# A conditional block for overflow jobs placed ahead of the last two scatters, and layer 1's accumulators in the branches moved to other PSUM tags

## The chip, the cores and the metric

The kernel runs on one core of a Trainium2 chip. The metric is the device time of one execution in microseconds (us), lower is better. Engines are named as in the profile: PE (TensorE; PEld is its weight load), DVE (VectorE), ACT (ScalarE), POOL (GpSimd), SP (SyncE, which only issues transfers here). A "q" behind a name (POOLq) is the engine's sequencer, which issues the instructions, waits on semaphores and takes branches.

## The reference

Retention attention (4 batches, 8 heads, 768 positions, head width 64) gives 3072 rows of 512. They go through a mixture of 8 experts in which each row takes the one expert with the highest logit:

```python
logits = x @ w_gate                       # 3072 x 8
expert_idx = np.argmax(logits, axis=1)
gate_w = softmax(logits)[row, expert_idx]
for e in range(E):                        # rows lo:hi of expert e, after sorting by expert
    h = np.maximum(x_sorted[lo:hi] @ w1[e], 0.0)    # 512 -> 1024
    y_sorted[lo:hi] = h @ w2[e]                     # 1024 -> 512
y = gate_w[:, None] * y_sorted[inv_perm]
```

## The kernel before

The first part, up to about 139 us, is attention and routing. The rows of `x` go to a scratch tensor in DRAM; the routing tables say, for each expert, which rows to gather and to which output rows its results are scattered. Nothing of that part is changed.

The second part is a loop over the eight experts (`for e in range(E)`), written in a hand-made order on all engines (`tc.manual_schedule`). Each expert has up to 512 places. Per expert:

- `tc.Switch(which, ARMS, ...)` (L742) branches on the number of rows in steps of 8. Only PE and ACT have code in its arms. An arm is one call of `job`: eight times `layer1` (PE products `hp` at L215, then a ReLU by ACT at L217 that writes `hT`), then `layer2` (PE products `ye` at L228, then ACT copies and scalings at L233, L234 and L236) for the rows beyond the first 256. A tile with 65 to 96 rows is done in two pieces, and a piece of up to 32 rows is laid over four column groups: its ACT part is then four copies (L233) and one scaling (L234).
- After the switch, `pair` (L258 and following) does the first 256 rows of the expert before (from e = 2 on; after the last switch it runs twice, for experts 6 and 7) with one level of Strassen's scheme: seven products `yp` (L266) in three PSUM accumulators `ya`, `yb`, `yc`. ACT scales some of them (`m` at L281, `o` at L290), DVE combines the rest (L272).
- POOL scatters the finished tiles to the output with indirect DMAs (`scatter`, L298) and gathers the rows of the expert after next; DVE transposes them (L206) and prepares sums and differences for the next `pair`.

PSUM has eight banks, given out by tag: `sc` (2), `lg` (1), `tr` (3), `y` (2). In `pair`, `ya` and `yb` take `sc`, and `yc` takes `tr`. In `layer1` the tag goes by the number of the block `f`:

```python
    hp_tags = [("sc", 2), ("sc", 2), ("lg", 1), ("tr", 3)]
    ...
        hp = ps(*hp_tags[f % len(hp_tags)], "hp")[:, 0:n]
```

An instruction that takes a bank waits, through a semaphore, until the last reader of that bank is done. Each engine counts its finished instructions in one semaphore. Where the reader stands in a switch, the count at which it is done differs from arm to arm, and one wait stands for all arms.

At the very end there is a block that is run only if some expert has more than 512 rows (not so with these inputs): `with tc.If(more > 0): further_jobs()` (L774), with `more` read into a register on every engine at L746. Where the block is not run, each engine still has a few instructions in its place, which bring the semaphores to the values that the block would have left: event semaphores on all engines, and on POOL an `INC_SWDGE_SEM`, which first waits until every scatter before it has landed. L797 is the end of the program: SP waits for all transfers, each engine drains, and POOL collects the others in a barrier.

Of the kernel before, what the change touches and what calls it, by code (L numbers as in the profile page):

```python
# [52 lines left out]
def kernel(  # L53
# [11 lines left out]
    nc = tc.nc  # L65
    B, H, S, D = q.shape
    N, DM = out.shape
    E = w_gate.shape[1]
# [5 lines left out]
    W = 512  # L74
    TC = W // P
    EARLY = 256
# [9 lines left out]
    def ps(tag, bufs, name):  # L86
        return psum.tile([P, 512], F32, tag=tag, name=name, bufs=bufs)
# [119 lines left out]
                    xT[ts(g, L), :, 0 : n * P].rearrange("p a (t r i) -> p r t a i", r=Q, i=L)[:, r, :, :, :],  # L207
                    xs[ts(r, L), tiles[0] : tiles[0] + n, ts(g, P)].rearrange("p t (a i) -> p t a i", i=L))

    hp_tags = [("sc", 2), ("sc", 2), ("lg", 1), ("tr", 3)]  # L210

    def layer1(n, xT, w1t, hT, f):
        hp = ps(*hp_tags[f % len(hp_tags)], "hp")[:, 0:n]
        for dt in range(DT):
            nc.tensor.matmul(hp, lhsT=w1t[:, 0, dt, ts(f, P)], rhs=xT[:, dt, 0:n], start=(dt == 0),  # L215
                             stop=(dt == DT - 1))
        nc.scalar.activation(out=hT[:, f, 0:n], in_=hp, func=AF.Relu)  # L217
# [78 lines left out]
    def scatter(o, idx, tiles):  # L296
        for t in tiles:
            done = nc.gpsimd.indirect_dma_start(  # L298
                out=out[:, :], out_offset=bass.IndirectOffsetOnAxis(ap=idx[:, t : t + 1], axis=0), in_=o[:, t, :],
                in_offset=None, bounds_check=N - 1, oob_is_err=False)  # L300

            tc.declare_no_dep(done.ins, group="scatters", reason="other rows of the output")
            tc.add_to_no_dep_group("scatters", done.ins)
# [32 lines left out]
    with ExitStack() as actx:  # L336
# [231 lines left out]
        xTa = first.tile([P, DT, EARLY], F32, tag="xTa", name="xTa")  # L568
        xT1 = first.tile([P, DT, W], F32, tag="xT1", name="xT1")
        hTa = keep.tile([P, FT, EARLY], F32, tag="hTa", name="hTa")  # L570
        oa = keep.tile([P, EARLY // P, DM], F32, tag="oa", name="oa")
        rest = iter(())
        for n in range(len(steps)):
            if n + AHEAD < len(steps):
                load(n + AHEAD)
            if n == len(steps) - 3:
                wa = weights(first, 0)
# [27 lines left out]
        for t in range(HALF):  # L605
            tr = ps("tr", 3, "tre").rearrange("p (a t) -> p a t", a=DT)
# [2 lines left out]
            nc.vector.tensor_copy(xTa[:, :, ts(t, P)], tr)  # L609
        next(rest, None)  # L610
        for f in range(FT):
            layer1(EARLY, xTa, wa[0], hTa, f)
            if f in (0, 1, 3):
                next(rest, None)
            if f == 2:
                ne = count()
        src, dst, gates = tables(inv, "", lambda rows: [gather(xs2[e], rows[:, ts(e, TC)], range(HALF, TC)) for e in range(2)])
        cols = [(src[:, ts(e, TC)], dst[:, ts(e, TC)], gates[:, ts(e, TC)]) for e in range(E)]
        arm, over = arms(ne)
# [14 lines left out]
    o2 = [keep2.tile([P, TC, DM], F32, tag=f"o{i}", name=f"o{i}") for i in range(2)]  # L634
# [23 lines left out]
        return xT  # L658

    def further_jobs():  # L660

        with tc.tile_pool(name="op", bufs=1) as op:

            def ot(shape, name, dt=F32):
                return op.tile(shape, dt, tag=name, name=name)


            jobs_i, jobs, jend, jbeg = ot([P, E], "jobs_i", I32), ot([P, E], "jobs"), ot([P, E], "jend"), ot([P, E], "jbeg")
            nc.vector.tensor_scalar(out=jobs_i, in0=ne, scalar1=float(W - 1), scalar2=float(W), op0=ALU.add, op1=ALU.max)
            nc.vector.tensor_single_scalar(jobs_i, jobs_i, W.bit_length() - 1, op=ALU.arith_shift_right)  # L670
            nc.vector.tensor_scalar(out=jobs, in0=jobs_i, scalar1=-1.0, scalar2=None, op0=ALU.add)
            ones_e = ot([P, E], "ones_e")
            nc.gpsimd.memset(ones_e, 1.0)
            nc.vector.tensor_tensor_scan(jend, ones_e, jobs, 0.0, op0=ALU.mult, op1=ALU.add)
            nc.vector.tensor_tensor(out=jbeg, in0=jend, in1=jobs, op=ALU.subtract)
            nth = ot([P, OV], "nth")
            nc.gpsimd.iota(nth, pattern=[[1, OV]], base=0, channel_multiplier=0, **exact)
            mine, whose_f, whose = ot([P, NT, E], "mine"), ot([P, OV], "whose_f"), ot([P, OV], "whose", I32)
            past = mine[:, 0:OV, :]
            nc.vector.tensor_tensor(out=past, in0=inner(nth[:, :], E), in1=middle(jend[:, :], OV), op=ALU.is_ge)  # L680
            nc.vector.tensor_reduce(whose_f, past, axis=AX.X, op=ALU.add)
            nc.vector.tensor_scalar(out=whose, in0=whose_f, scalar1=float(E - 1), scalar2=None, op0=ALU.min)


            blk, jf, big = ot([P, NT], "blk", I32), ot([P, NT], "jf"), ot([P, NT], "big")
            nc.vector.tensor_single_scalar(blk, ranks, W.bit_length() - 1, op=ALU.arith_shift_right)
            nc.vector.tensor_tensor(out=mine, in0=ohs, in1=middle(jbeg[:, :], NT), op=ALU.mult)
            nc.vector.tensor_reduce(jf, mine, axis=AX.X, op=ALU.add)
            nc.vector.tensor_tensor(out=jf, in0=jf, in1=blk, op=ALU.add)
            nc.vector.tensor_scalar(out=big, in0=blk, scalar1=1.0, scalar2=None, op0=ALU.is_ge)  # L690
            nc.vector.tensor_tensor(out=jf, in0=jf, in1=big, op=ALU.mult)
            nc.vector.tensor_scalar(out=jf, in0=jf, scalar1=-1.0, scalar2=None, op0=ALU.add)
            col, prow = ot([P, NT], "ocol", I32), ot([P, NT], "oprow", I32)
            nc.vector.tensor_single_scalar(prow, ranks, P - 1, op=ALU.bitwise_and)
            nc.vector.tensor_single_scalar(col, ranks, W - 1, op=ALU.bitwise_and)
            nc.vector.tensor_single_scalar(col, col, P.bit_length() - 1, op=ALU.arith_shift_right)
            slot, slots = ot([P, NT], "slot"), ot([P, OV * TC], "slots")
            nc.gpsimd.iota(slots, pattern=[[1, OV * TC]], base=0, channel_multiplier=0, **exact)
            nc.vector.scalar_tensor_tensor(out=slot, in0=jf, scalar=float(TC), in1=col, op0=ALU.mult, op1=ALU.add)
            at = ot([P, NT, OV * TC], "oat")  # L700
            val = ot([P, NT, 5, OV * TC], "oval", BF16)
            nc.vector.tensor_tensor(out=at, in0=middle(slots[:, :], NT), in1=inner(slot[:, :], OV * TC), op=ALU.is_equal)

            for i in range(5):
                nc.vector.tensor_tensor(out=val[:, :, i, :], in0=at, in1=inner(told[:, :, i], OV * TC), op=ALU.mult)
            here = ot([P, NT, P], "ohere", BF16)
            nc.vector.tensor_tensor(out=here, in0=middle(rrow[:, :], NT), in1=inner(prow[:, :], P), op=ALU.is_equal)
            found = ps("tr", 3, "ofound")[:, 0 : 5 * OV * TC]
            for n in range(NT):
                nc.tensor.matmul(found, lhsT=here[:, n, :], rhs=val[:, n, :, :].rearrange("p a s -> p (a s)"),  # L710
                                 start=(n == 0), stop=(n == NT - 1))
            got = ot([P, 5, OV * TC], "got")
            nc.vector.tensor_copy(got[:, :, :].rearrange("p a s -> p (a s)"), found)
            osrc, odst, ogates = tables(got, "_o")
            fetch = [nc.sync.value_load(whose[0:1, j : j + 1], min_val=0, max_val=E - 1) for j in range(OV)]
        for j, ev in enumerate(fetch):
            w1t, w2t = weights(first, ev)
            xT = mp.tile([P, DT, W], F32, tag="xTs", name="oxT")
            hT = mp.tile([P, FT, W], F32, tag="hT", name="ohT")
            gather(xs2[j % 2], osrc[:, ts(j, TC)], range(TC))  # L720
            turn(xs2[j % 2], xT, range(TC))
            for f in range(FT):
                layer1(W, xT, w1t, hT, f)
            for t in range(TC):
                layer2(W, hT, w2t, o2[j % 2], t, ogates[:, ts(j, TC)])
            scatter(o2[j % 2], odst[:, ts(j, TC)], range(TC))

    with tc.manual_schedule(engines={PE, ACT, POOL, DVE, SP}):
        for t in o2:
# [3 lines left out]
        for e in range(E):  # L733
# [8 lines left out]
            for a in tc.Switch(which, ARMS, hint=f"job{e}"):  # L742
                n = max(STEP * (LEAST + a) - (0 if e else EARLY), STEP)
                job(n, xT, w1s[e], w2s[e], hT, o2[e % 2], cols[e][2], HALF if e else 0, hint if e < 2 else lambda: None)
            if last:
                more = nc.values_load(over[0:1, 0:1], min_val=0, max_val=1)  # L746
            else:
                xT, which = xTn, nxt
            if last:
                end = halves_of_h(hT, mp.tile([P, DT, W], F32, tag="xTs", name="xTs")), end  # L750
            for d in [e - 1] * (e > 1) + [e] * last:
                pair(hTs[d], w2s[d], *(end if d == e else sums), o2[d % 2], cols[d][2],
                     lambda: None if last else hint())
                if d < e:
                    scatter(o2[e % 2], cols[e][1], range(HALF, TC))
                scatter(o2[d % 2], cols[d][1], [1, 0])
                if d + 2 < E:
                    w2s.append(weights2(homes[d % 2], d + 2))
# [10 lines left out]
            if e + 2 < E:  # L769
                xTn = rows_of(e + 2)  # L770
            if e + 2 == E:

                end = halves_of_w(w2s[E - 1], [x[:, 2 * i : 2 * i + 2, :].rearrange("p a d -> p (a d)") for x in xs2 for i in range(2)])
    with tc.If(more > 0):  # L774
        further_jobs()


# [23 lines left out]
```

## Time and profile before

| what | value |
|---|---|
| four runs | 490.22, 490.65, 491.77 and 495.67 us; median 491.21 |
| profiled execution | 490.91 us; span from first to last instruction 489.0 us |
| granted TensorE clock, mean | 0.992 |
| PE busy, whole span | 465.1 us (95%) |
| PE busy, 184 to 300 us | 116.0 of 116 us |
| PE busy, 300 to 340 us | 37.95 of 40 us |
| PE busy, 340 to 478 us | 137.18 of 138 us |
| PE busy, 478 to 489 us | 0 of 11 us |
| POOL busy, 478 to 489 us | 0.98 us |

The first row says how far runs lie apart; the second ties the trace to a time: 1.9 us lie outside the span. The rows by stage say where PE has no gap (so that only less PE work or a faster PE would help) and where it has.

### The profile page before, as it was taken

To read this page: it belongs to the slowest core of one execution; us is meant where nothing else is said; L and a number is where in the kernel's file an instruction comes from. 1 tells how busy PE (TensorE), PEld (TensorE's weight loads), DVE (VectorE), ACT (ScalarE), POOL (GpSimd) and SP (SyncE) were. 2 spreads that over 40 slices of the span, in tenths; PEclk is the share of its full clock that TensorE was granted. 3 is DMA by queue.
4 is the path that set the end of the run, shared out by engine and by line. 5 is a ranking of instruction groups with operands and counts; after the bars stand their busy time and mean duration, and the time that the engine had idled before them with its cause. 6 is when DMAs were issued, how large, how long until landed. Compare 5 with 4: busy or idle time off the path is not lost.

```text
span 489.0 us, 8236 instructions
## 1 busy us (share of the span) xinstructions
PE 465.1 (95%) x3238; PEld 320.1 (65%) x3238; DVE 260.2 (53%) x551; ACT 106.4 (22%) x218; POOL 133.8 (27%) x132
## 2 busy tenths in 40 slices
PE   7999999998989999999999999989999999999990
PEld 4778778786767565555585557658557766755880
DVE  3468776787778920765525714383481636550310
ACT  2343333332221112212211120131131121012110
POOL 2772533441303124033026012411501511100211
PEclk9999999999999999999999999999999999999996
DMA  9998999792961089343009202901910570320011
GB/s 210 217 229 204 225 236 218 171 199 70 340 195 41 25 300 364 132 135 133 3 28 353 93 26 78 380 17 39 365 56 30 168 290 21 123 95 3 26 46 46
DMA packets 93498, 72.52 MB, mean 148 GB/s; under 512 B 53466, under 2 KB 78042, under 8 KB 93408
## 3 DMA queue, kind: packets, MB, share of 16 engines
q1 hardware_dynamic: 88144, 58.74, 42.3%
q0 software_dynamic: 5120, 12.60, 7.3%
q8 instruction: 48, 0.79, 0.7%
q14 instruction: 42, 0.34, 0.2%
q10 hardware_dynamic: 144, 0.05, 0.0%
HBM read 60.88 MB, written 14.68 MB: 155 GB/s over the span
## 4 chain that ended last, share of the span: by engine, by line
PE 85%; DVE 9%; ACT 1%; issue 1%; DMA 1%; POOL 0%; SPq 0%; DVEq 0%; POOLq 0%; ACTq 0%
PE hp L215 35%; PE yp L266 17%; PE ye L228 16%; PE y L440 4%; PE sc L411 4%; DVE am L413 3%; PE tr L371 2%; PE y L435 2%; PE new L422 2%; PE warm L344 1%; DVE xg L447 1%; DMA x_d<-xg 1%; PE parts L459 1%; DVE told L522 1%; PE lgp L469 1%
## 5 line engine op out<-in xcount | busy, mean ns | idle before, releaser
L215 PE MATMUL hp<-xTs,w1t 128*128 128x392 f32 (+5 forms) x384 | 127.4, 492 | 0.0
L215 PEld LDWEIGHTS hp<-xTs,w1t 128*128 128x128 f32 x384 | 73.0, 190 | 52.5 <-issue 30.1
L206 DVE STREAM_TRANSPOSE xTs<-xs 32x512 f32<-32x512 f32 x96 | 67.5, 703 | 62.9 <-DMA xs<-x_d,src 36.3
L298 POOL DMA_INDIRECT out_dram<-o,dst x30 | 33.9, 1129 | 228.2 <-ACT o L236 135.3
L228 PE MATMUL ye<-w2t,hT 128*8 128x128 f32 (+6 forms) x496 | 66.4, 360 | 0.0
L217 ACT ACTIVATE hT<-hp 128x392 f32<-128x392 f32 (+6 forms) x64 | 29.2, 468 | 143.0 <-PE hp L215 116.5
L228 PEld LDWEIGHTS ye<-w2t,hT 128*8 128x8 f32 (+6 forms) x496 | 32.6, 123 | 31.6 <-issue 29.0
L165 POOL DMA_INDIRECT xs<-x_d,src x28 | 37.6, 1343 | 24.6 <-DVE at L188 16.4
L413 DVE TENSOR_TENSOR am<-sc,causal 128x512 f32<-128x512 f32 x48 | 30.7, 681 | 17.9 <-PE sc L411 17.9
L272 DVE SCALAR_TENSOR_TENSOR u<-yp,gate,m 128x256 f32<-128x256 f32 x14 | 6.8, 484 | 57.3 <-ACT m L281 29.7
L385 POOL TENSOR_TENSOR vs<-v,dec 128x512 f32<-128x512 f32 x23 | 24.5, 1069 | 32.1 <-PE y L440 16.2
L266 PE MATMUL yp<-ws,hs 128*128 128x256 f32 x144 | 32.1, 379 | 0.0
L440 PE MATMUL y<-am,vs 128*64 128x128 f32 x384 | 29.3, 279 | 2.6 <-DVE am L413 2.2
L382 POOL TENSOR_TENSOR qs<-q,dec 128x512 f32<-128x512 f32 x22 | 22.5, 1044 | 29.4 <-DMA q<-in_q_dram 29.4
L266 PEld LDWEIGHTS yp<-ws,hs 128*128 128x128 f32 x144 | 27.4, 190 | 3.7
L411 PE MATMUL sc<-qT,kT 64*128 64x128 f32 x384 | 27.9, 285 | 1.4 <-ACT qT L399 0.7
L266 PE MATMUL yp<-w2t,hT 128*128 128x256 f32 x112 | 26.5, 380 | 2.0 <-ACT o L234 2.0
L440 PEld LDWEIGHTS y<-am,vs 128*64 128x64 f32 x384 | 22.0, 136 | 8.2 <-DVE am L413 4.1
L411 PEld LDWEIGHTS sc<-qT,kT 64*128 64x128 f32 x384 | 23.3, 187 | 5.2 <-issue 2.7
L266 PEld LDWEIGHTS yp<-w2t,hT 128*128 128x128 f32 x112 | 21.2, 190 | 7.3 <-issue 2.4
L442 ACT COPY xTg<-y 128x512 f32<-128x512 f32 x24 | 14.1, 587 | 49.5 <-PE y L440 44.5
L215 PE MATMUL hp<-xTa,w1t 128*128 128x256 f32 (+1 forms) x128 | 22.5, 330 | 0.8 <-DVE xTa L609 0.5
(169 smaller groups left out, 525.7 us busy)
## 6 DMA issues: line engine op xcount, KB each, us to landing
w1t<-in_moe_w_dram SPq DMA_DIRECT2D x8, 2048.0 KB, 17.6
w2t<-in_moe_w_dram SPq DMA_DIRECT2D x8, 2048.0 KB
k<-in_k_dram SPq DMA_DIRECT2D x24, 256.0 KB, 5.2
q<-in_q_dram SPq DMA_DIRECT2D x12, 512.0 KB, 7.0
v<-in_v_dram SPq DMA_DIRECT2D x24, 256.0 KB, 5.7
x_d<-xg SPq DMA_DIRECT2D x24, 256.0 KB, 4.3
out_dram<-o,dst POOLq DMA_INDIRECT x30, 3.3
xs<-x_d,src POOLq DMA_INDIRECT x28, 4.7
```

The costliest lines, as they stand in the source:

```text
L165: nc.gpsimd.indirect_dma_start(out=xs[:, t, :], out_offset=None, in_=x_d[0:rows, :], in_offset=bass.IndirectOffsetOnAxis(ap=idx[:, t : t + ...
L206: nc.vector.transpose(xT[ts(g, L), :, 0 : n * P].rearrange("p a (t r i) -> p r t a i", r=Q, i=L)[:, r, :, :, :], xs[ts(r, L), tiles[0] : t ...
L215: nc.tensor.matmul(hp, lhsT=w1t[:, 0, dt, ts(f, P)], rhs=xT[:, dt, 0:n], start=(dt == 0), stop=(dt == DT - 1))
L217: nc.scalar.activation(out=hT[:, f, 0:n], in_=hp, func=AF.Relu)
L228: nc.tensor.matmul(y[j * z : j * z + m, 0:c], lhsT=hT[:, f, t * P + r0 : t * P + r0 + m], rhs=w2t[:, 0, f, ts(j, c)], start=(f == 0), stop ...
L266: nc.tensor.matmul(y, lhsT=a[:, f, :], rhs=b[:, f, :], start=start and f == 0, stop=f == FH - 1, skip_group_check=True)
L298: done = nc.gpsimd.indirect_dma_start(out=out[:, :], out_offset=bass.IndirectOffsetOnAxis(ap=idx[:, t : t + 1], axis=0), in_=o[:, t, :], i ...
L382: mul.tensor_tensor(out=qs[:, e, :, :], in0=got["q"][:, :, ts(e, D)], in1=inner(dec[:, ts(c + e, H)], D), op=ALU.mult)
L385: mul.tensor_tensor(out=vs, in0=got["v"], in1=inner(dec[:, ts(NC + c, H)], D), op=ALU.mult)
L411: nc.tensor.matmul(sc[j][:, a, :], lhsT=kT[r, a, :], rhs=qT[r, a, :], start=True, stop=True)
L413: nc.vector.tensor_tensor(out=am[j], in0=sc[j], in1=middle(causal[:, :], HP), op=ALU.mult)
L440: nc.tensor.matmul(y[ts(j, D), a, :], lhsT=vs[:, 2 * a + j, :], rhs=am[j][:, a, :], start=(c == 0), stop=True, skip_group_check=True)
```

## The change

Three edits:

1. `layer1` has an argument with its tags. Inside the branches it takes `lg`, `tr`, `tr`, `tr` in turn; the one call outside (the first 256 rows of expert 0, ahead of the loop) passes the old list.
2. `further_jobs()` and its `tc.If` stand inside the last turn of the loop, after the last `pair` and ahead of the last two scatters, with `preferred_fallthrough_block=False`, which puts the code of the case "not run" directly behind the compare and the block behind that. `further_jobs` uses the output tile `o2[E % 2]`, that is `o2[0]`, which the last two scatters (of `o2[1]`) don't read.
3. `more` is read at the end of the turn e = 6 rather than after the last switch.

```diff
-    hp_tags = [("sc", 2), ("sc", 2), ("lg", 1), ("tr", 3)]
-
-    def layer1(n, xT, w1t, hT, f):
-        hp = ps(*hp_tags[f % len(hp_tags)], "hp")[:, 0:n]
+    def layer1(n, xT, w1t, hT, f, tags=(("lg", 1), ("tr", 3), ("tr", 3), ("tr", 3))):
+        hp = ps(*tags[f % len(tags)], "hp")[:, 0:n]
...
-            layer1(EARLY, xTa, wa[0], hTa, f)
+            layer1(EARLY, xTa, wa[0], hTa, f, (("sc", 2), ("sc", 2), ("lg", 1), ("tr", 3)))
...
-                layer2(W, hT, w2t, o2[j % 2], t, ogates[:, ts(j, TC)])
-            scatter(o2[j % 2], odst[:, ts(j, TC)], range(TC))
+                layer2(W, hT, w2t, o2[E % 2], t, ogates[:, ts(j, TC)])
+            scatter(o2[E % 2], odst[:, ts(j, TC)], range(TC))
...
-            if last:
-                more = nc.values_load(over[0:1, 0:1], min_val=0, max_val=1)
-            else:
+            if not last:
                 xT, which = xTn, nxt
...
                 if d < e:
                     scatter(o2[e % 2], cols[e][1], range(HALF, TC))
+                if d == e:
+                    with tc.If(more > 0, preferred_fallthrough_block=False):
+                        further_jobs()
                 scatter(o2[d % 2], cols[d][1], [1, 0])
...
             if e + 2 == E:
+                more = nc.values_load(over[0:1, 0:1], min_val=0, max_val=1)
...
-    with tc.If(more > 0):
-        further_jobs()
```

## Prediction

> **What bounds the kernel now.** First the busy time by stage (columns: us, then busy time and count of PE, PEld, DVE, ACT, POOL, then clock, DMA share, GB/s):
>
> ```profile
> 300.00:340.00 40.00, 37.95 (x223) 27.69 (x222) 21.23 (x30) 8.22 (x19) 11.04 (x9) 1.00 0.41 146
> 340.00:478.00 138.00, 137.18 (x595) 91.08 (x593) 61.32 (x85) 22.81 (x49) 28.31 (x23) 1.00 0.31 112
> 478.00:489.00 11.00, 0.00 (x0) 0.00 (x0) 0.00 (x0) 0.00 (x0) 0.98 (x1) 0.62 0.11 41
> ```
>
> In the loop over the experts PE is the bound: it has no gap from 340 us to its end at 477.2, at a granted clock of 1.00. An edit that takes no PE work away can gain in two places only: the 2.05 us that PE misses between 300 and 340 us, and the 11 us after PE's end, in which one 0.98 us instruction is all that any engine computes.
>
> The timeline shows the first place (start, length, engine, line, operation, count, idle before and who ended it):
>
> ```profile
> 320.51 5.56 PE L228 MATMUL ye<-w2t,hT 128*64 128x256 f32 x96
> 326.14 1.10 ACT L233 COPY o<-ye 32x128 f32<-32x128 f32 x4 [0.39 <-PE ye L228]
> 327.27 0.72 ACT L234 ACTIVATE o<-o,gate 32x512 f32<-32x512 f32 x1
> 328.12 1.97 PE L266 MATMUL yp<-w2t,hT 128*128 128x256 f32 x8 [2.05 <-ACT o L234]
> ```
>
> PE ends expert 4's arm at 326.07 and starts the pair at 328.12, when ACT has done the five last instructions of its own arm. The pair doesn't read what these write. It takes the `sc` banks, last read by ReLUs of the arm, long done; but one wait value stands for all arms, and in the arm that ran it is reached only by ACT's last instruction. In the other arms no such gap is seen: they end in one ACT instruction (L236), and PE goes on at once.
>
> The second place, by the instructions of L774 (the conditional) and L797 (the end of the program) after 470 us; columns: count, shortest/median/longest in ns, first and last start:
>
> ```profile
> L774 POOLq EVENT_SEMAPHORE  x5: 17/43/43, 478.7 to 481.3; - x5
> L774 PEldq COMPARE_BRANCH  x1: 3358/3358/3358, 473.2 to 473.2; - x1
> L774 DVEq COMPARE_BRANCH  x1: 67/67/67, 477.2 to 477.2; - x1
> L774 POOLq COMPARE_BRANCH  x1: 50/50/50, 478.2 to 478.2; - x1
> L774 POOLq INC_SWDGE_SEM  x1: 1459/1459/1459, 481.4 to 481.4; - x1
> ```
>
> ```profile
> L797 SPq EVENT_SEMAPHORE  x14: 17/28/28, 482.8 to 488.9; - x14
> L797 POOLq DRAIN  x3: 40/107/5298, 482.9 to 488.7; - x3
> L797 SPq DRAIN  x3: 7/7/7, 483.5 to 488.4; - x3
> L797 PEldq DRAIN  x2: 8/8/8, 477.4 to 488.5; - x2
> ```
>
> And POOL's timeline:
>
> ```profile
> 466.38 0.98 POOL L298 DMA_INDIRECT out_dram<-o,dst  x1 [1.24 <-issue]
> 476.25 0.98 POOL L298 DMA_INDIRECT out_dram<-o,dst  x1 [8.88 <-DVE o L272]
> 478.47 0.98 POOL L298 DMA_INDIRECT out_dram<-o,dst  x1 [1.24 <-issue]
> ```
>
> So the tail is: last scatter 478.47 to 479.45; landed at 481.3 (2.8 after its start); INC_SWDGE_SEM 1.46 to 482.8; POOL's first DRAIN 5.30, from 482.9 to 488.2; barrier and clean-up to 489.0 (0.8). SP, which waits for the same transfers, passes its list from 482.8 to 483.5 and is then kept by POOL's DRAIN. PE was at its own DRAIN at 477.4.
>
> **The change part by part.**
>
> *Tags of layer 1.* The order of instructions as built shows that the pair's first products no longer wait for ACT; the wait stands at the third product, where `yc` takes a `tr` bank. Two products lie ahead of it: 16 records of 0.216 (12.09 us for 56 of them in the chain of waits) are 3.45 us. For expert 4 that is 326.07 + 3.45 = 329.5, and ACT's arm ends at 327.99: hidden with 1.5 to spare. DVE's last transpose ends at 328.7, before its first instruction of the pair can start (329.5). ACT's scaling of `ya`, ready at 327.8, is 0.2 late, which nobody waits for. So 2.05 us go. If the cover of 3.45 were gone, the stall would only move: 0 saved. Bounds 0 and 2.05; I take 2.05. In the arms, layer 1 still turns over four banks, so each product waits for the ReLU four blocks back, as before; `yc`'s old bank is met at the fourth block, some 8 us after DVE has read it. What comes after, products, gathers and weight loads, starts 2.05 earlier with it: the next expert's rows were ready (328.7) and its weights asked for (302.1) long before 338.4.
>
> *Reading `more` earlier.* On PE it is one TENSOR_LOAD of 0.32 and two register instructions ahead of the last switch, where the other turns read their arm number (0.31) and PE shows no gap. On ACT 0.28, on DVE 0.54 ahead of differences needed 30 us later. Nothing, hidden behind PE's queue of products. Without that cover: 0.5.
>
> *The conditional ahead of the last two scatters.* PE, DVE and ACT have nothing behind it. On POOL the two scatters are queued behind it. POOL's part (compare, waits, INC) can start when the scatter of 466.38 has landed, 469.2, and takes 1.46, to 470.7; the next scatter needs DVE's result of 476.0. POOL idles 8.88 us there, so the move is hidden; cover left, 5.3. If the cover were gone, the last scatter would slip by what is over.
>
> What it brings at the end depends on what the 5.30 of DRAIN belongs to; no other row shows this DRAIN behind a scatter, so I bound it:
> - (a) It belongs to DRAIN itself, whatever came before. It then starts when the last scatter is issued, 479.45 in place of 482.86: 3.4 us less, span 485.6.
> - (b) It is work that INC leaves behind on POOL. It moves with INC to 470.7 to 476.0, just ahead of DVE's result, and the end is set by SP: landed 481.3, some 0.6 for the rest of SP's list, 0.8 for the barrier: 482.7, 6.3 less.
> - (c) It starts only when all scatters have landed: 481.3 + 5.3 + 0.8 = 487.4, 1.6 less.
> - Below (c), nothing: 489.0.
>
> I take (a): INC's row has ended, SP has seen its increments by 482.8, and DRAIN's row is one of its own.
>
> [...] The case "not run" now ends in a jump over the whole block on every engine, on PE only after its last product. The trace's rows for it are 3.36 on PE at L774, 4.56 for PE's longest branch at L797, and at most 0.08 on ACT, DVE and POOL. [...]
>
> *Sum,* on the profiled execution's own 490.91 us (span 489.0 and 1.9 around it): 490.91 − 2.05 − 3.41 = 485.4. That execution lies 0.3 below the median of the runs shown, 491.21.
>
> **The rivals.**
> - *(b), DRAIN's 5.3 goes with INC.* For it: the program's start has a DRAIN of 0.19 before any scatter, and those after the long one are 0.11 and 0.04, so DRAIN alone is short. Against it: INC's increments are out before DRAIN starts. 490.91 − 2.05 − 6.3 = 482.6.
> - *(c), DRAIN waits for the landing.* For it: in the trace it started with everything landed, so its 5.3 may contain no waiting. Against it: INC had waited for the landing already, and nothing shows that DRAIN does. 490.91 − 2.05 − 1.6 = 487.3.
> - *The tail gives nothing:* the end is kept at 489.0 by something else, and only PE's gap goes: 488.9. Against it: no other engine is active there.
> - *Slower: the conditional holds POOL's last two scatters.* Let POOL be free of it at T. Two scatters in a row start 0.98 + 0.30 apart (0.30 is the row at 455.62), the second lands 2.8 later, and with (c)'s DRAIN and barrier the span ends at T + 1.28 + 2.8 + 5.3 + 0.8 = T + 10.2. After PE's gain of 2.05 this is more than 489.0 from T = 480.9 on. [...] Against it: POOL's branches take 0.05 at most and the next POOL row follows within 0.4.
>
> **How the numbers follow.** Chances: (a) 0.34, (b) 0.28, (c) 0.20, no gain at the tail 0.08, slower 0.05, others 0.05. The likeliest gives 485.4; its own range, with 0 to 2.05 for the tags, is 485 to 487.5. The range that leaves out less than 2 in 10 reaches from (b), 482.6, to the case without a gain at the tail, 488.9: 482.0 to 489.2. A measurement of this kernel can tell about 1% from no change; 1% below 491.21 is 486.3. (a) and (b) lie under it: 0.6 with a little off for the tags. (c), no gain at the tail and the slower rival at its 495.2 lie within 1%: 0.35 with what is left. Slower by over 1% (496.1) takes one fetch more than the slower rival counts, or something that the trace doesn't show: 0.05.
>
> **What would show it right or wrong.** Right: no idle time of PE before the first pair product of expert 4; INC_SWDGE_SEM near 467 (469.2 less 2.05), ahead of two scatters whose distance from PE's end is as before (last one 1.3 us after it); a POOL DRAIN of about 5.3 that starts when the last scatter's row ends. DRAIN short and the end 3.3 after the last scatter's row: (b). DRAIN ending 5.3 after the last landing: (c). Wrong altogether: the last scatter more than 2 us after PE's end, or new idle time of PE at the third product of a pair or inside an arm.

## The result, and the profile after

The changed kernel takes 489.09 us (median of 45 runs, 486.68 to 494.0) against 491.52 (71 runs of the kernel before, 489.14 to 495.67): ratio 0.9951, 95% interval 0.9938 to 0.9965, so 2.4 us less (1.7 to 3.0). The prediction's 485.4 was 5.5 less on its profiled execution and 5.8 below the median that it had. Its profiled execution took 487.64 us with a span of 485.9, that is 3.27 and 3.07 less than the one before.

Busy time by stage, in the changed kernel (us, then busy time and count of PE, PEld, DVE, ACT, POOL, clock, DMA share, GB/s):

```profile
300.00:340.00 40.00, 38.40 (x224) 27.94 (x223) 21.17 (x31) 8.22 (x19) 11.54 (x9) 1.00 0.40 146
340.00:478.00 138.00, 136.81 (x592) 90.57 (x590) 61.19 (x85) 22.83 (x49) 27.81 (x22) 1.00 0.31 111
```

Between 300 and 340 us PE still misses 1.60 us. Between 340 us and its end at 477.50 it now misses 0.69, where it missed nothing. The timeline shows both places. At the end of expert 4's arm:

```profile
320.33 5.56 PE L226 MATMUL ye<-w2t,hT 128*64 128x256 f32 x96
325.95 1.10 ACT L231 COPY o<-ye 32x128 f32<-32x128 f32 x4 [0.39 <-PE ye L226]
327.08 0.71 ACT L232 ACTIVATE o<-o,gate 32x512 f32<-32x512 f32 x1
327.49 1.99 PE L264 MATMUL yp<-w2t,hT 128*128 128x256 f32 x8 [1.60 <-issue]
```

PE starts the pair before ACT is done (327.79), so it no longer waits for ACT; but it idles 1.60 us all the same, now for "issue", that is for no wait that the trace knows. And ahead of expert 6's first product:

```profile
381.33 1.89 PE L264 MATMUL yp<-w2t,hs 128*128 128x256 f32 x8
383.91 1.45 PE L213 MATMUL hp<-xTs,w1t 128*128 128x360 f32 x4 [0.69 <-issue]
```

What stands in both places is a branch of PE's own sequencer. The line of the compares (L797 before, L796 after) shows it. Columns: count, shortest/median/longest in ns, first and last start. The kernel before, 324 to 329 us, and then 380 to 386 us:

```profile
L797 PEldq COMPARE_BRANCH  x1: 2697/2697/2697, 325.3 to 325.3; - x1
...
L797 PEldq COMPARE_BRANCH  x1: 393/393/393, 380.8 to 380.8; - x1
```

The changed kernel, 324 to 329 us and 379 to 386 us:

```profile
L796 PEldq COMPARE_BRANCH  x1: 2357/2357/2357, 325.1 to 325.1; - x1
...
L796 PEldq COMPARE_BRANCH  x1: 3457/3457/3457, 380.2 to 380.2; - x1
```

At expert 4 it is the branch out of the arm: it ended at 327.95 before (2.70 after 325.26) and at 327.43 after (2.36 after 325.07), and the pair's first product came 0.17 and 0.06 later. ACT's last instruction ended at 327.99 before, within 0.04 of PE's branch; the experiments below show that this was chance. At expert 6 it is the branch into the arm, 3.46 us long where it was 0.39.

The end of the program, by the conditional (L754) and the end (L796), in the same columns:

```profile
L754 POOLq EVENT_SEMAPHORE  x5: 17/43/43, 466.6 to 469.6; - x5
L754 PEldq COMPARE_BRANCH  x2: 101/1949/3797, 473.5 to 477.8; - x2
L754 POOLq INC_SWDGE_SEM  x1: 1415/1415/1415, 469.7 to 469.7; - x1
```

```profile
L796 POOLq DRAIN  x3: 40/113/6512, 478.6 to 485.7; - x3
L796 SPq DRAIN  x3: 7/7/7, 482.5 to 485.3; - x3
L796 PEldq DRAIN  x2: 8/36/65, 481.6 to 485.4; - x2
```

and POOL's timeline:

```profile
466.70 0.98 POOL L296 DMA_INDIRECT out_dram<-o,dst  x1 [1.24 <-POOLq L754]
476.57 0.98 POOL L296 DMA_INDIRECT out_dram<-o,dst  x1 [8.88 <-DVE o L270]
478.79 0.98 POOL L296 DMA_INDIRECT out_dram<-o,dst  x1 [1.24 <-issue]
```

INC_SWDGE_SEM lies in POOL's idle time, from 469.71 to 471.12. The DRAIN's row begins at 478.57, a little before the last scatter's, and ends at 485.08: 5.31 after the scatter's end (479.78), as it ended 5.33 after INC's end before. From the start of the last scatter to the span's end it is 7.13 us in place of 10.52: 3.39 less, with the last scatter 1.30 after PE's end (1.29 before).

The span's 3.07 add up: 3.39 at the tail and 0.38 ahead of the loop (first product at L213 at 138.94 in place of 139.32, in code that is the same), less 0.70 that the loop up to PE's end is longer (338.56 in place of 337.86). Of this 0.70, the smaller gap at expert 4 gives −0.45 and expert 6 +0.93, counted from the first product of the pair ahead of its arm to the first product of its layer 2 (32.38 in place of 31.45); the other 0.2 came ahead of expert 4.

### The profile page after: what moved, and what is told of

The parts are those of the page before. It is cut to its first block, busy times and chain, and to the rows that moved or that the text cites. A ratio compares the mean times of both kernels' runs of the same rounds, so it can differ in the third digit from the quotient of the medians.

```text
span 485.9 us, 8229 instructions
## 1 busy us (share of the span) xinstructions
PE 464.7 (96%) x3238; PEld 319.4 (66%) x3238; DVE 259.2 (53%) x551; ACT 106.4 (22%) x218; POOL 133.8 (28%) x132
## 4 chain that ended last, share of the span: by engine, by line
PE 83%; DVE 9%; DMA 3%; issue 2%; ACT 1%; POOLq 0%; SPq 0%; ACTq 0%; POOL 0%; DVEq 0%
PE hp L213 34%; PE yp L264 17%; PE ye L226 16%; PE y L438 3%; PE sc L409 3%; DVE am L411 3%; PE tr L369 2%; PE y L433 2%; PE new L420 2%; DMA xs<-x_d,src_e 2%; DMA q<-in_q_dram 1%; DVE xg L445 1%; DMA x_d<-xg 1%; DVE here L534 1%; PE parts L457 1%
## 5 line engine op out<-in xcount | busy, mean ns | idle before, releaser
L213 PE MATMUL hp<-xTs,w1t 128*128 128x392 f32 (+5 forms) x384 | 127.5, 493 | 0.7 <-issue 0.7
L213 PEld LDWEIGHTS hp<-xTs,w1t 128*128 128x128 f32 x384 | 72.8, 190 | 53.9 <-issue 31.2
L213 PE MATMUL hp<-xTa,w1t 128*128 128x256 f32 (+1 forms) x128 | 22.5, 330 | 0.3 <-ACT hT L215 0.2
```

## The experiments

The theory from the two traces: *the branch*, that is, PE's gap at expert 4 was never ACT's, and the new gap at expert 6 is PE's branch into the arm, longer since the arm's code stands at another place. The rival: *the wait*, that is, the gap was ACT's and turned into something else, and the new gap comes from the new tags' waits. All kernels beside each other (the gap is PE's idle time ahead of the first product, in brackets PE's branch; tail is from the start of the last scatter to the span's end; times in us; a rerun bears the name of the kernel that it repeats; gaps, branches and tail are from one profiled execution each, and kernels with one run have no interval):

| kernel | median (runs) | ratio to before, 95% | expert 2 | expert 4 | expert 6 | tail |
|---|---|---|---|---|---|---|
| before | 491.52 (71) | | 0 | 2.05 (2.70) | 0 (0.39) | 10.52 |
| whole change | 489.09 (45) | 0.9951 (0.9938 to 0.9965) | 0 | 1.60 (2.36) | 0.69 (3.46) | 7.13 |
| e9, whole change | 488.25 (9) | 0.9938 (0.9913 to 0.9962) | 0 | 1.68 (2.44) | 0.50 (3.26) | 7.13 |
| e1, conditional alone | 486.89 (9) | 0.9918 (0.9890 to 0.9946) | 0 | 1.77 (2.42) | 0 (0.29) | 7.13 |
| e12, as e1 | 487.93 (12) | 0.9935 (0.9911 to 0.9959) | 0 | 1.69 (2.33) | 0 (0.39) | 7.13 |
| e15, as e1 | 487.66 (11) | 0.9931 (0.9904 to 0.9957) | 0 | 2.11 (2.76) | 0 (0.39) | 7.12 |
| e2, tags alone | 492.79 (12) | 1.0023 (0.9998 to 1.0047) | 0 | 1.94 (2.70) | 0.54 (3.30) | 10.51 |
| e3, change + reversed pieces | 486.22 (6) | 0.9891 (0.9860 to 0.9922) | 1.47 | 0 (1.43) | 0.56 (3.32) | 7.13 |
| e4, e1 + reversed pieces | 486.85 (6) | 0.9890 (0.9857 to 0.9924) | 1.48 | 0 (1.21) | 0 (0.31) | 7.13 |
| e13, as e4 | 484.78 (5) | 0.9867 (0.9845 to 0.9889) | 0 | 0 (1.46) | 0 (0.30) | 7.13 |
| e10, change, code shifted by 20 | 488.10 (12) | 0.9941 (0.9916 to 0.9965) | 0 | 1.97 (2.73) | 0 (0.29) | 7.13 |
| e11, e1, code shifted by 236 | 487.56 (1) | | 0 | 1.77 (2.42) | 0.60 (3.29) | 7.13 |
| e14, e10 + reversed pieces | 486.41 (7) | 0.9917 (0.9885 to 0.9950) | 1.58 | 0 (1.21) | 0 (0.41) | 7.13 |
| e5, change, no conditional | 487.63 (1) | | 0 | 1.58 (2.34) | 0.74 (3.49) | 7.08 |
| e6, e1 + late ACT | 493.01 (1) | | 0 | 4.87 (2.58) | 0 (0.30) | 7.13 |
| e7, change + late ACT | 489.74 (1) | | 0 | 1.70 (2.46) | 0.14 (2.73) | 7.13 |
| e8, change, no last scatters | 485.48 (1) | | 1.44 | 1.60 (2.36) | 1.00 (3.76) | |

**The two parts apart: e1_tail (old tags, conditional moved) and e2_tags (new tags, conditional at the end).**

```diff
-    def layer1(n, xT, w1t, hT, f, tags=(("lg", 1), ("tr", 3), ("tr", 3), ("tr", 3))):
+    def layer1(n, xT, w1t, hT, f, tags=(("sc", 2), ("sc", 2), ("lg", 1), ("tr", 3))):   # e1
```

```diff
-                if d == e:                                                             # e2
-                    with tc.If(more > 0, preferred_fallthrough_block=False):
-                        further_jobs()
...
+    with tc.If(more > 0):
+        further_jobs()
```

> Only the conditional and the reading of `more` are moved; layer 1 keeps the old tags in the branches. Theory A (the tail gives all the gain; PE's return branch from expert 4's arm, not ACT, holds the pair): last scatter to end of span 7.1 us as with the whole change, PE's gap ahead of expert 4's pair 1.5 to 2.1 us, time 0.4 to 0.7% below before, the same as the whole change within 0.2%. Rival B (the tags give 0.5 us or more of the gain): 0.5 us or more slower than the whole change, gap 2.05.

> Only the tags of layer 1 in the branches are changed; the conditional stays at the end. Theory A: gap ahead of expert 4's pair 1.5 to 2.0 us, tail from the last scatter to the end of the span 10.5 us as before, time within 0.2% of before. Rival B (the tags free the pair, and the whole change lost it again through the moved conditional): gap under 0.5 us, time 0.4% below before.

The whole gain at the tail is the conditional's: 7.13 in e1 and 10.51 in e2. The tags alone gain nothing (1.0023). The gap at expert 4 is there with either tags, 1.69 to 2.11 with the old ones (before, e1, e11, e12, e15) and 1.58 to 1.97 with the new ones (the change, e2, e5, e7 to e10), and the gap at expert 6 comes with the new ones. e1 gained somewhat more than expected: 0.8% in place of 0.4 to 0.7. e2's profile was also taken with half the clock from 328.0 to 331.5 us, right behind the gap at expert 4 (of the others only e6, below, shows the like), so its span is not set beside the others'. The third number from the end is the clock:

```profile
328.00:331.50 3.50, 3.50 (x10) 2.79 (x9) 0.33 (x1) 0.45 (x2) 1.86 (x2) 0.51 0.19 60
331.50:334.00 2.50, 2.50 (x13) 2.19 (x13) 0.48 (x1) 0.39 (x2) 0.00 (x0) 1.00 0.03 7
```

**Branch or wait at expert 4: e3_rev_new and e4_rev_old.** The 65 to 96 rows of a tile are done small piece first (with the new tags, and with the old tags; the conditional is moved in both). The arm of expert 4 then ends in 32 products that are longer than the 64 short ones (in e4 the 64 take about 1.9 us and the 32 about 3.7, by the starts of their weight loads, 323.02 and 324.91, and PE's end at 328.59), so that PE's sequencer gets to its branch further ahead of PE (2.3 us in place of 0.8), while ACT's part of the last piece ends later than PE.

```diff
-        for r0, m in [(0, P // 2), (P // 2, m - P // 2)] if P // 2 < m <= P * 3 // 4 else [(0, m)]:
+        for r0, m in [(P // 2, m - P // 2), (0, P // 2)] if P // 2 < m <= P * 3 // 4 else [(0, m)]:
```

> The whole change, and in a tile of 65 to 96 rows the small piece is done ahead of the piece of 64 rows, so that expert 4's arm ends in 32 longer PE records rather than 64 short ones: PE's sequencer is further ahead when it reaches the branch. Theory A: the branch still takes 2.4 to 3 us, but the gap ahead of the pair falls from 1.6 to 0.7 to 1.1 us. Rival C (the gap is a wait of the pair's first product, for ACT or a transfer): it stays at 1.5 us or more. Time 0 to 0.2% below the whole change.

> As the run before, with the old tags in the branches. ACT's arm then ends in two copies and a scaling, 1.5 us after PE's last product of the arm. If the old tags made the pair wait for ACT's last instruction: gap 1.6 to 1.8 us, 0.7 us or more above the new tags in the same order. Theory A in its strict form (the wait value was reached some instructions before ACT's end and never bound): gap as with the new tags in the same order, 0.7 to 1.1 us.

The gap is gone in both, with the old tags too, and in e4 the pair starts while ACT has 1.6 us of its arm still to do. Its timeline and its branch out of the arm:

```profile
323.03 5.56 PE L226 MATMUL ye<-w2t,hT 128*32 128x128 f32 x96
...
328.51 1.78 PE L264 MATMUL yp<-w2t,hT 128*128 128x256 f32 x7
328.63 0.76 ACT L231 COPY o<-ye 64x256 f32<-64x256 f32 x2 [1.74 <-PE ye L226]
329.42 0.72 ACT L232 ACTIVATE o<-o,gate 64x512 f32<-64x512 f32 x1
```

```profile
L796 PEldq COMPARE_BRANCH  x1: 1210/1210/1210, 326.3 to 326.3; - x1
```

The pair starts at 328.51 while ACT's last instruction runs to 330.14. So the old tags' wait does not hold PE until ACT's arm ends. The branch starts at 326.3, 2.2 us before the pair, and takes 1.2: PE has no gap there. In the order before it started 0.8 us ahead (325.26 against 326.07) and took 2.70. That is the 2.05, with the 0.17 to the first product.

The expectations had the branch at 2.4 to 3 us and a gap of 0.7 to 1.1, so the new order did more than expected, and it did two things. PE's sequencer reaches the branch 2.3 us ahead of the end of the arm's last product in all four profiles of the new order, and 0.8 in all thirteen of the old. And the branch is shorter, 1.2 to 1.5 us in place of 2.3 to 2.8. The trace has packets of 16,384 bytes in a DMA queue that its table names "instruction" (q8: 48 packets, 0.79 MB in the kernel before). One of them starts 1.2 to 1.3 us ahead of this branch in the new order and within 0.3 us of its start in the old, and in all seventeen profiles the branch ends 2.3 to 2.8 us after that packet has started.

Both show a new gap of 1.5 at 215 us, ahead of expert 2's first product, behind a branch at 207 that took 4.8 where it takes 2.3 to 3.5 otherwise. Whether that belongs to the reversed pieces is taken up with e13.

**Place of the code or waits at expert 6: e9_again, e10_pad, e11_shift, e12_tail_again.** In the built code PE's program has 31 instructions fewer with the new tags than before, and expert 6's arm that runs starts at instruction 57274 in place of 57294. e10 brings it back to 57294 with the new tags, by five products in an arm of expert 5 that isn't run. e11 brings it to 57530 = 57274 + 256 with the old tags, by 59 such products. The compare of this switch stands 3253 instructions ahead of the arm in all of them, so it moves along. e9 and e12 repeat the whole change and e1 on the same chip.

```diff
             for a in tc.Switch(which, ARMS, hint=f"job{e}"):
                 n = max(STEP * (LEAST + a) - (0 if e else EARLY), STEP)
+                if e == 5 and n == 424:
+                    hp = ps("lg", 1, "hp")[:, 0:n]          # e11: ps("sc", 2, "hp")
+                    for _ in range(5):                      # e11: 59
+                        nc.tensor.matmul(hp, lhsT=w1s[e][:, 0, 0, 0:P], rhs=xT[:, 0, 0:n], start=True, stop=True)
```

> The whole change once more, on the same chip as the kernels with shifted code. All theories: span about 486; last scatter to the span's end 7.1 us; expert 4's gap of PE 1.4 to 2.0 with PE's branch of L796 at 325 taking 2.4 to 2.7; expert 6's gap 0.5 to 0.7 at 383 with PE's branch there taking 3.3 to 3.5. Ratio to before 0.994 to 0.997.

> The whole change with five extra products in one arm of expert 5 that isn't run with these inputs (424 rows). They take 20 of PE's instructions, so that expert 6's switch and arms stand in PE's code at the same instruction as in the kernel before (the arm that runs starts at instruction 57294 in place of 57274); nothing that runs is changed. Theory 'place of the code': expert 6's gap of 0.5 to 0.7 us goes, PE's branch there takes 0.3 to 0.5 as in the kernel before, the time is 0.5 to 0.7 us below the whole change's. Theory 'waits of the new tags': branch 3.3 to 3.5 and gap 0.5 to 0.7 as in the whole change, same time.

> The other way round: old tags, the conditional moved, and 59 extra products in the same arm of expert 5 that isn't run, which put expert 6's arm at instruction 57530, that is 256 behind the whole change's 57274. Theory 'place of the code, in blocks of 256 instructions': the branch at expert 6 takes 3.3 to 3.5 us and PE gets a gap of 0.5 to 0.7, with the old tags. Theory 'waits of the new tags': branch at most 0.5, no gap. If the distance of the jump decides rather than the place in a block (3253 instructions from compare to arm in all of them), neither follows and the branch is short.

> Old tags with the conditional moved, once more beside the whole change. All theories: no gap at expert 6, tail 7.1, so 0.5 to 1.5 us less than the whole change, ratio to before 0.990 to 0.994.

The place decides, both ways. e10's branch into expert 6's arm, and then e11's:

```profile
L800 PEldq COMPARE_BRANCH  x1: 294/294/294, 381.3 to 381.3; - x1
```

```profile
L800 PEldq COMPARE_BRANCH  x1: 3287/3287/3287, 380.2 to 380.2; - x1
```

With the new tags at the old place the branch is short and the gap is gone; with the old tags 256 instructions behind the new place it is long and the gap is there (0.60). The packets of the instruction queue go with it: in e10 one runs from 377.36 to 378.38 and ends 3 us ahead of the branch; in e9 one runs from 381.27 to 382.27, 0.9 after the branch (380.34) has begun. It is so in all seventeen profiles: in the nine with a short branch a packet starts 3.8 to 4.1 us ahead of it, in the eight with a long one (2.7 us and more) none does, and one starts 0.2 to 1.0 us after the branch has begun. A packet doesn't name its engine, and no row says what it brings. I read these times so that the arm's code came ahead of the branch in the one place and during it in the other.

The length of the jump does not set the duration: the arm lies 3253 instructions behind the compare in both places, and the branch took 0.29 us in e10 and 3.29 in e11.

Why a packet comes ahead of the branch in one place and not in the other stays open. A BRANCH_PREFETCH_HINT of PE's sequencer stands ahead of the branch in both (at 373.87 in e10, at 372.92 in e9), so the hint alone does not decide it. Whether the place of the arm or that of the compare decides is not shown, since no run moves one without the other.

In the time this can't be told, though 0.5 to 0.7 us (e10) and 0.5 to 1.5 (e12) below the whole change were expected: e10's ratio lies on e9's, and e9's (0.9938) on e12's (0.9935). In the profiles it can. From the first product of the pair ahead of expert 6's arm to the first product of its layer 2, PE takes 31.45 us in all nine profiles with the short branch. With the long one it takes 32.18 in e9, 32.38 in the first profile of the whole change and 32.18 to 32.69 in all but e7 (31.83, where the branch took 2.73). So the long branch costs 0.7 to 1.2 us here, somewhat more than the gap in the table, which is counted from a modelled end.

The loop up to PE's end, from the first product of L213 (expert 0's first 256 rows, ahead of the loop proper), takes 338.32 in e9, 337.54 in e10, 337.20 in e12; it contains the differences at expert 4 and elsewhere too. The start of this stretch lies between 137.87 and 140.41 from one profiled execution to another, in code that is the same in all of them, and so varies by more than this difference.

**What the old wait is worth: e6_late_old and e7_late_new.** Twelve more copies at the end of ACT's arm of expert 4, with the old tags (conditional moved) and the new.

```diff
                 nc.scalar.activation(out=o[rows, t, :], in_=o[rows, t, :], func=AF.Copy, scale=gate[rows, t : t + 1])
+                if r0 and parts == 4:
+                    for _ in range(12):
+                        nc.scalar.copy(out=ident[rows, :], in_=o[rows, t, 0:P])
```

> Old tags, the conditional moved, and twelve more copies of ACT (about 0.28 us each, into a constant tile that nobody reads any more) at the end of the arms that end in a piece of up to 32 rows, of which expert 4's is the only one that runs. ACT's arm of expert 4 then ends at about 331.4 in place of 328.0, PE's at 326 as before. Theory A (the pair's first product waits until ACT is at the end of its arm): gap of PE about 5.3, or about 4.4 if the value waited for is reached some instructions before the end. Theory B (the wait never counts, PE's branch alone makes the gap): gap 1.7 to 2.0 as in the kernel without the copies.

> The whole change with the same twelve copies of ACT at the end of expert 4's arm (ends at about 331.4). Theory A and the instruction order: the first two products go on after the branch (gap 1.4 to 2.0 at 326), the third, due 3.45 us later at about 331.0, waits 0 to 0.5 us for ACT. So the new tags are worth 3 to 4 us here, and nothing where ACT is as fast as it is. Theory B: same gap as the old tags' version, and no gap at the third product.

Old tags, from the timeline:

```profile
320.84 5.56 PE L226 MATMUL ye<-w2t,hT 128*64 128x256 f32 x96
328.32 3.87 ACT L235 COPY ident<-o 32x128 f32<-32x128 f32 x12
331.27 3.78 PE L267 MATMUL yp<-w2t,hT 128*128 128x256 f32 x8 [4.87 <-ACT ident L235]
```

So the wait exists: with ACT late, PE stands 4.87 us. But it is not for the last instruction. The pair starts at 331.27, when the ninth of the twelve copies is done (a copy every 0.325; the ninth from 330.92 to 331.21), three ahead of the end. Carried over to the kernel before, where ACT's arm ended in four copies and one scaling, the wait was met by the second copy, at 326.68, 1.3 us ahead of the end of PE's branch (327.95). By this reading it could have held PE for 0.6 us at most, and held it for none.

New tags:

```profile
327.81 1.99 PE L267 MATMUL yp<-w2t,hT 128*128 128x256 f32 x8 [1.70 <-issue]
328.03 3.87 ACT L235 COPY ident<-o 32x128 f32<-32x128 f32 x12
329.64 3.65 PE L267 MATMUL yp<-ws,hs 128*128 128x256 f32 x16
...
334.26 0.84 ACT L282 ACTIVATE m<-yp,gate 128x256 f32<-128x256 f32 x2 [2.37 <-issue]
334.77 0.48 DVE L273 SCALAR_TENSOR_TENSOR u<-yp,gate,m 128x256 f32<-128x256 f32 x1 [6.12 <-ACT m L282]
...
335.31 1.99 PE L267 MATMUL yp<-ws,hs 128*128 128x256 f32 x8 [2.02 <-DVE u L273]
```

Three products go on behind the branch, as the instruction order says, and the third waits for nothing to speak of. The expectation of 3 to 4 us missed the fourth: it needs DVE's `u2`, which needs ACT's scaling, and that starts at 334.26 only (2.37 us of "issue" after the last copy; what ACT does in them is not shown). The stall moves: 4.87 becomes 1.70 + 2.02, so that even with ACT 3.9 us late the new tags save 1.2 of idle time. e6's loop is longer than e7's by more, 342.99 against 340.01, and behind its longer gap the clock stood at half, while e7's stayed at 1.00. e6 by stages:

```profile
331.00:333.00 2.00, 1.73 (x4) 1.47 (x5) 0.00 (x0) 1.09 (x4) 0.53 (x1) 0.50 0.02 4
333.00:335.00 2.00, 2.00 (x6) 1.55 (x6) 0.00 (x0) 0.00 (x0) 1.49 (x2) 0.50 0.25 93
335.00:336.50 1.50, 1.50 (x6) 1.21 (x5) 0.00 (x0) 0.84 (x2) 0.00 (x0) 0.60 0.08 17
```

**What the DRAIN belongs to: e8_no_last and e5_no_if.** The whole change without the last two scatters, and without the conditional and its read.

```diff
-                scatter(o2[d % 2], cols[d][1], [1, 0])
+                scatter(o2[d % 2], cols[d][1], [] if d == e else [1, 0])                 # e8
...
-                if d == e:                                                               # e5
-                    with tc.If(more > 0, preferred_fallthrough_block=False):
-                        further_jobs()
...
-                more = nc.values_load(over[0:1, 0:1], min_val=0, max_val=1)
```

> The whole change without the last two scatters (256 rows of the last expert stay unwritten). Theory 'POOL's DRAIN takes 5.3 us after the last indirect transfer': the last one is now at 467 to 469, so the DRAIN is over soon after POOL reaches it; the span ends by PE's last branch (about 3.8 us from 477.5 to 481.5, as the last engine at the barrier) and the 0.8 of the barrier, so 482.3 to 482.6. Theory 'DRAIN takes 5.3 us whenever it starts': POOL gets there at about 471 or at 477.5, so the span ends at 482.5 (hidden behind PE) or at about 483.6.

> The whole change without the conditional block and without the read of its condition (an expert with more than 512 rows would be left short; there is none). Theory 'the moved conditional is hidden': last scatter to the span's end stays 7.1 us, with the DRAIN 5.3 behind the last scatter, and PE reaches its own DRAIN at 477.6 rather than 481.6, which changes nothing; span 485.5 to 486. If PE's late DRAIN or INC_SWDGE_SEM still holds the end: tail 0.3 to 1 us shorter.

e8, by the lines of the end and of the conditional:

```profile
L796 POOLq DRAIN  x3: 40/107/5219, 473.3 to 483.5; - x3
...
L796 PEldq DRAIN  x2: 8/36/65, 482.9 to 483.3; - x2
```

```profile
L754 PEldq COMPARE_BRANCH  x2: 104/1765/3426, 475.2 to 479.4; - x2
```

The last scatter ended at 469.39 here, INC at 472.83, and the DRAIN still took 5.22 from 473.27 on. So it is not the time since the last indirect transfer: the second theory. It is hidden then, and PE's branch ends last: PE's last product ends at 479.20, its branch at 482.82, the span at 483.77. (PE's end is 1.7 later than in the whole change, mainly since this profile has gaps of 1.44 at expert 2 and 1.00 at expert 6.) e5:

```profile
L791 POOLq DRAIN  x3: 40/107/6505, 478.6 to 485.6; - x3
```

No INC_SWDGE_SEM and no conditional, and the DRAIN ends at 485.10, 5.30 after the last scatter's end; with a tail of 7.08 in place of 7.13 and the same span. So the moved conditional costs 0.05 us at the tail, and the loop, with the earlier read of `more` gone too, is 338.41 in place of 338.56. The DRAIN's 5.2 to 5.3 us are not INC's either. What POOL does in them stays open: its DRAINs right behind take 0.11 and 0.04.

**The better version, and the gap of expert 2: e13_rev_again (e4 again), e14_pad_rev (e10 and e3 in one), e15_tail_again (e1 again), on one chip.**

```diff
-        for r0, m in [(0, P // 2), (P // 2, m - P // 2)] if P // 2 < m <= P * 3 // 4 else [(0, m)]:
+        for r0, m in [(P // 2, m - P // 2), (0, P // 2)] if P // 2 < m <= P * 3 // 4 else [(0, m)]:   # e13, e14
...
+                if e == 5 and n == 424:                     # e14, with five products as in e10
```

> Old tags, conditional moved, small piece ahead of the large one: once more. If expert 2's gap of 1.4 us at 215 belongs to one execution in several (it was also seen in the kernel without the last two scatters, whose pieces are in the old order), it need not come back; then the loop takes PE about 336 us from its first product to its end, 1.5 less than in the kernel with the conditional alone. If it belongs to the order of the pieces, it comes back with PE's branch at 207 taking 4.8. No gap at expert 4 in either case; ratio to before 0.987 to 0.992.

> The whole change with both of PE's gaps taken out: the five products in the arm that isn't run, and the small piece ahead of the large one. No gap at expert 4, none at expert 6, tail 7.1. Ratio to before 0.987 to 0.992, that is the same as with the old tags: with the branches out of the way the new tags are worth nothing here.

> Old tags with the conditional moved alone, beside the two versions without a gap at expert 4: 1.5 to 2 us more than they, gap of 1.6 to 2.0 at 326.

e13 has none of the three gaps and its loop takes 335.55 us, e15's 337.62 with its gap of 2.11. It beats both kernels: 0.9867 (0.9845 to 0.9889) against 0.9931 (0.9904 to 0.9957) for e15 on the same chip, and 0.9951 for the whole change. The first measurement of the same two kernels (e4, 0.9890, and e1, 0.9918, on one chip) points the same way with intervals that overlap. Expert 2's gap came in e4 and not in e13, which are the same kernel, and came in e8, whose pieces are in the old order. So the order of the pieces does not make it by itself. e14's profile has it too (1.58). In these four profiles two packets of the instruction queue start 0.3 to 0.7 us apart, just after PE's branch at 207 has begun, and the branch takes 4.8 to 4.9; in the other thirteen the second packet comes over 3 us later. What brings the two packets together stays open. Three of the four are among the four profiles of the new order and one among the thirteen of the old, which is too few to settle whether the order makes it likelier.

e14's loop of 337.24 less that gap is 335.66, within 0.11 of e13's 335.55, so with both branches out of the way the new tags are worth nothing in the loop. Its time, expected to be e13's, was 1.6 us above it; whether its other executions had the gap too is not shown. e15, expected 1.5 to 2 us above both, was 2.9 above e13 and 1.3 above e14.

## Why the prediction was right or wrong

- **Conditional: right.** Case (a) gave 3.41 at the tail; 3.39 came. INC lay in POOL's idle 8.88 us as said. (b) falls by the DRAIN staying long after INC was moved or taken out (after, e5); (c) by its end, 5.3 after the scatter's row, not after the landing (3.2 after the scatter's start). What in POOL the 5.3 belong to, the runs don't say. The slower rival needed POOL to be held until 480.9; POOL left the conditional at 471.2. Its 495.2 adds two stays of POOL as long as PE's longest branch, 4.56 each, and the 496.1 one more (a fetch); no run shows such a stay: in the changed kernel POOL's two branches of the conditional took 0.03 and 0.05 us.
- **PE's branch over the block: a cost that stayed hidden.** The jump took 3.80 us from 477.78, between the rows 3.36 and 4.56 that the prediction gives for it, and PE reached its DRAIN at 481.6, 3.5 ahead of the end of POOL's (485.08). e8 shows what it costs once that cover is gone: it then sets the end (branch to 482.82, span 483.77).
- **Reading `more` earlier: right,** nothing, by e5.
- **Tags: wrong, and this is the step that failed.** "PE ... starts the pair at 328.12, when ACT has done the five last instructions of its own arm" took the order of two events for a cause, and "in the arm that ran it is reached only by ACT's last instruction" was never read from a row (by e6 it is reached three instructions ahead of the end). The 2.05 was PE's own branch. I read PE's longest branch of L797, 4.56, for the end of the program alone, and did not ask where the other branches of that line stood: one of 2.70 ended 0.17 before the pair's first product. The remark that the other arms show no gap, put down to their ending in one ACT instruction, had the same other reading: they don't end in 64 short products, and the sequencer is further ahead at the branch (in the kernel before by 7.1 us at expert 5, branch at 364.63 and arm's end at 371.74, and by 6.3 at expert 6, 403.75 and 410.06). The sign that the prediction named, no idle time of PE ahead of expert 4's pair, did not come: 1.60 us were left. The term is 0, not 2.05: of the 0.45 that the gap at 326 shrank, 0.34 is a branch of 2.36 in place of 2.70, within what that branch took in other kernels (2.33 to 2.76, with either tags).
- **A cost that the prediction did not have:** the tags change the number of PE's instructions, which moves every later arm, and expert 6's lands at 57274, where PE's branch into it took 3.46 us in place of 0.39: 0.9 us in the profile of the result, 0.7 in e9.
- **The sum** by what was measured: 490.91 − 3.39 + 0.7 to 0.9 = 488.2 to 488.4 on the profiled execution, 2.5 to 2.7 less, which lies in the measured interval (1.7 to 3.0). The top of the likeliest case's own range, 487.5, was the case with nothing from the tags; the cost at expert 6 lies beyond it. The measured median, 489.09, lies beside 488.9, the number of the rival in which the tags give all and the tail nothing. That is chance: it was the other way round, and both medians lie above their profiled executions (491.52 against 490.91, 489.09 against 487.64).

## What to carry to other kernels

When an engine idles right behind a branch, put its own sequencer's branch row beside the gap before believing an inferred releaser; two events that end within 0.1 us of each other need an experiment that parts them. In these traces a branch on PE costs its duration less how far the sequencer is ahead of PE (2.70 less 0.81 in the kernel before, with a gap of 2.05; 1.21, with 2.2 us ahead, left none in e4), so it paid here to end an arm in long products, not in many short ones: a changed order of two pieces was worth, in the loop, the 2 us that new accumulators were meant to bring (335.55 in e13 against 337.62 in e15), though in three of its four profiles a gap of 1.5 elsewhere took most of it back. And an edit that adds or removes instructions anywhere ahead of a switch moves the code behind it (here by 20 instructions, and PE's branch at expert 6 went from 0.39 to 3.46 us): compare the branch rows of all later switches, not only the place that was edited.

## What was not expected of the hardware

- POOL's first DRAIN at the end of the program took 5.30 us (before) and 5.22 (e8) behind INC_SWDGE_SEM, and it ended 5.31 us (after) and 5.30 (e5) behind the last scatter where that came last.
- PE's branch into expert 6's arm took 0.29 to 0.41 us where a packet of 16,384 bytes started 3.8 to 4.1 us ahead of it, and 2.7 to 3.8 where one started 0.2 to 1.0 us after it; the packet itself took 1.0 to 1.4 us.
- At expert 6 this goes with the place of the code, whichever tags: long with the arm at instruction 57274 (3.46 in the whole change, 3.26 in e9) and at 57530 (3.29, e11), short at 57294 (0.39 before, 0.29 in e10). No other distance than these 20 and 256 instructions was run.
- PE's sequencer reached the branch out of expert 4's arm 0.8 us ahead of PE when 64 short products ended the arm, and 2.3 us ahead when 32 longer ones did, in every profile.
- The clock went to 0.51 for 3.5 us behind a gap of 1.94 us (e2) and to 0.50 for 5 us (331 to 336) behind one of 4.87 (e6), while gaps of 1.97 (e10) and 2.11 (e15) at the same place left it at 1.00. e6's loop took 2.98 us more than e7's, with 1.15 us more of idle time at expert 4.
